# Issuing four small loads ahead of the entry barrier, beside the first two long ones

## The chip, the cores and the metric

The kernel runs on one core of a Trainium2 chip. The metric is the device time of one execution in microseconds. The kernel before takes 381.84 us (median of three runs, 381.80 to 381.89).

## The reference, cut to what matters

One decode step: attention of 32 query heads over a cache of 65,536 keys and values in 4 groups, and a gated mixer, both fed by the same row `x` of 1024 elements, and blended by a gate.

```python
g = _sigmoid((x * gate_w).sum(-1, keepdims=True))        # x and gate_w: 1024 elements each
a = _A_ref(x, A_k_cache, A_v_cache, A_wq, A_wo)          # x @ wq, scores, softmax, p @ v, @ wo
b = _B_ref(x, B_w_in, B_w_sp, B_b_sp, B_w_out)           # gelu, layernorm, * w_sp + b_sp, @ w_out
return g * a + (1 - g) * b
# ... the functions are left out; the sequence length is 1, so w_sp and b_sp are one number each
```

The weights and caches are 162 MB, all of which must be read once. `x`, `gate_w`, `w_sp` and `b_sp` together are about 4 KB.

## The kernel before

A recorder notes every operation with what it reads and writes, works out the waits, and emits each engine's instructions in program order. The long loads are issued by SP; those two that need no free slot are moved ahead of the entry barrier, the point near the start at which all engines wait for one another (`R.ahead = 2`). What one engine issues stands in one row of packets, which 16 transfer engines carry. A load is known to have landed by its semaphore: after its data, each transfer engine that took part sends a packet of 4 bytes, which the trace records like the others.

```python
        run("SP", nc.sync)
        # ...
        made = list(body.instructions)
        moved = made[first:first + self.ahead]
        body.instructions = made[:gate] + moved + made[gate:first] + made[first + self.ahead:]
        run("POOL", nc.gpsimd)
        run("PE", nc.tensor)
        run("ACT", nc.scalar)
        run("DVE", nc.vector)
```

The four small loads are ACT's first instructions, behind the barrier:

```python
    def small(dst, src, key):
        # ...
        P("ACT", f, w=[key], dma="l" + key)
    # ...
    small(xrow[0:8, 0:128], A_x[0, 0].rearrange("(i n) -> i n", i=8), KX)        # x: 8 rows of 256 bytes
    small(grow[0:8, 0:128], gate_w.rearrange("(i n) -> i n", i=8), KG)           # gate: the same
    small(wb[0:1, 0:1], B_w_sp, "wsp")                                           # 2 bytes
    small(wb[0:1, 1:2], B_b_sp.rearrange("(a n) -> a n", a=1), "bsp")            # 2 bytes
```

The long loads, in their order (8 MB, 8 MB, 7 MB and so on). A load is issued when the ring slots under it have been used up; `w_in` takes the slots of `wq`:

```python
    load([("wq", 0)], rows(A_wq, 0, 8), VB)
    load_k2(0, 0)
    load([("win", 0)], rows(B_w_in, 0, 8), VB)
    load_k(2, 2)
    # ... 25 more
```

PE's program in the first stage, in order: `x` turned into columns, the matmul that spreads `w_sp` and `b_sp`, the gate's matmul, then 64 matmuls on `wq`, after which the slots are free.

```python
    P("PE", f, r=["xm", "oneb"], w=[KTB])                      # x into columns
    # ...
    P("PE", lambda e: e.matmul(mb[:, 0:2], oneb[0:1, :], wb[0:1, :], start=True, stop=True),
      r=["oneb", "wsp", "bsp"], w=["mb"])
    # ... DVE: product of x and gate, its sum
    P("PE", lambda e: e.matmul(tb[:, 0:1], ones[0:8, :], col(C_GS)[0:8, :], start=True, stop=True),
      r=["ones", "gs"], w=[KTB])
    # ... the sigmoid
    wqs, keys = use(("wq", 0))
    # ...
    P("PE", f, r=["xT"] + keys, w=["ob"])                      # x @ wq
    done(("wq", 0))                                            # lets w_in be issued
```

## Time and profile before

| | before |
|---|---|
| time, us | 381.84 |
| span of the profile, us | 380.5 |
| share of the 16 transfer engines taken by the long loads | 98.8% |
| busiest compute engine | PE, 61% |
| last small load (`b_sp`) landed, us | 21.96 |
| first `wq` matmul, us | 23.51 |
| `w_in` issued, us | 29.46 |
| first keys transposed, us | 41.19 |

The third and fourth rows name the bound: bytes. The last four are the first stage, the one that the change touches. The lines of the page and of the timeline that show all this are in the prediction below. One view is not there: who waited for whom in the first 42 us of the kernel before (columns: total us, times, longest us).

```profile
PE mbt L430 <- DMA arena<-in_B_b_sp_dram: 10.5, 1, 10.5
...
DVE arena L495 <- DMA arena<-in_A_k_cache_dram: 9.0, 1, 9.0
...
DVE arena L420 <- DMA arena<-in_A_x_dram: 5.0, 1, 5.0
```

Three waits for transfers stand here. Two are for small loads, 10.5 and 5.0 us. The one in the middle, for the first keys, comes after both.

### The profile page before, as it was taken

How to read it: one execution, taken by the hardware profiler on the slowest of the kernel's cores; microseconds unless marked ns; L12 is line 12 of the kernel's file. 1: busy time of each engine (PE TensorE's matmuls, PEld its weight loads, DVE VectorE, ACT ScalarE, POOL GpSimd, SP SyncE). 2: the span in 40 equal slices, each digit the busy share in tenths (PEclk: the TensorE clock that was granted, in tenths of full speed). 3: DMA queues.
4: the chain of work that ended last, by engine and by line, in shares of the span. 5: the costliest groups of instructions: out<-in, count | busy, mean ns of one | idle time of the engine just before them, and what ended most of it. 6: DMA issues, size and time to landing. Idle time of an engine off the chain costs nothing.

```text
span 380.5 us, 2581 instructions
## 1 busy us (share of the span) xinstructions
PE 231.1 (61%) x1449; PEld 57.7 (15%) x836; DVE 204.1 (54%) x162; ACT 23.2 (6%) x24; POOL 8.4 (2%) x37
## 2 busy tenths in 40 slices
PE   0051488458548924894786128952895883738378
PEld 0010011011101200121111001220121110212015
DVE  3111596777389525955892249745875872322020
ACT  1000000010420000002100000022000000220010
POOL 5000000000000000000000000000000000000000
PEclk9998599696959985998799859995999897969789
DMA  9999999999999999999999999999999999999996
GB/s 441 434 406 400 469 388 437 441 483 417 415 406 434 441 436 427 441 420 424 474 434 441 441 441 406 408 434 441 434 417 432 441 441 434 436 410 431 417 424 252
DMA packets 4254, 162.17 MB, mean 426 GB/s; under 512 B 532, under 2 KB 532, under 8 KB 788
## 3 DMA queue, kind: packets, MB, share of 16 engines
q1 hardware_dynamic: 4208, 162.01, 98.8%
q8 instruction: 9, 0.15, 0.2%
q10 hardware_dynamic: 36, 0.00, 0.0%
q14 instruction: 1, 0.01, 0.0%
HBM read 162.01 MB, written 0.00 MB: 426 GB/s over the span
## 4 chain that ended last, share of the span: by engine, by line
DMA 57%; PE 21%; DVE 19%; ACT 1%; issue 1%; ACTq 0%; SPq 0%; DVEq 0%
DMA arena<-in_A_k_cache_dram 34%; DVE arena L495 17%; DMA arena<-in_A_wo_dram 10%; DMA arena<-in_A_v_cache_dram 8%; PE scp L253 5%; DMA arena<-in_B_b_sp_dram 5%; PE scp L255 5%; PE obt L253 4%; PE obt L255 4%; DVE arena L532 1%; PE fbt L705 1%; PE fbt L653 1%; ACT arena L527 1%; ACTq L281 0%; SPq L382 0%
## 5 line engine op out<-in xcount | busy, mean ns | idle before, releaser
L495 DVE STREAM_TRANSPOSE arena<-arena 128x2048 f32<-128x2048 f32 x64 | 142.6, 2281 | 45.4 <-DMA arena<-in_A_k_cache_dram 32.0
L253 PE MATMUL scp<-arena 128*128 128x512 bf16 (+1 forms) x275 | 110.7, 419 | 87.3 <-DVE arena L495 86.2
L255 PE MATMUL scp<-arena 128*128 128x512 bf16 (+1 forms) x279 | 110.5, 415 | 0.0
L253 PE MATMUL obt<-arena 128*64 128x512 bf16 (+2 forms) x334 | 62.3, 416 | 21.7 <-DMA arena<-in_A_v_cache_dram 20.3
L255 PE MATMUL obt<-arena 128*64 128x512 bf16 (+2 forms) x334 | 61.6, 411 | 0.0
L253 PEld LDWEIGHTS scp<-arena 128*128 128x128 bf16 (+1 forms) x275 | 27.3, 103 | 196.5 <-issue 96.9
L532 DVE STREAM_TRANSPOSE arena<-arena 128x2048 bf16<-128x2048 bf16 x7 | 16.2, 2311 | 30.1 <-PE obt L255 27.9
L253 PEld LDWEIGHTS obt<-arena 128*64 128x64 bf16 (+1 forms) x334 | 18.1, 112 | 74.3 <-issue 54.9
L527 ACT ACTIVATE arena<-arena 128x2048 bf16<-128x2048 f32 x8 | 16.0, 2002 | 218.7 <-DVE arena L524 195.8
L512 DVE TENSOR_SCALAR_CACHE_REDUCE arena<-scp 128x2048 f32<-128x2048 f32 x8 | 18.3, 2292 | 16.0 <-PE scp L255 16.0
L573 PE MATMUL mbt<-arena 128*128 128x128 bf16 x16 | 1.8, 243 | 12.6 <-DVE arena L568 12.6
L561 DVE RECIPROCAL arena<-mbt 128x1 f32<-128x1 f32 x4 | 0.6, 139 | 15.8 <-PE mbt L556 15.8
L524 DVE TENSOR_REDUCE arena<-mbt 128x1 f32<-128x32 f32 x4 | 0.8, 192 | 15.3 <-PE mbt L521 15.3
L483 POOL COPY arena<-arena 32x32 bf16<-32x32 bf16 x16 | 3.2, 203 | 235.5 <-PE scp L255 209.4
L535 DVE STREAM_TRANSPOSE arena<-arena 128x1024 bf16<-128x1024 bf16 x2 | 2.5, 1245 | 11.0 <-PE obt L255 11.0
L425 PE MATMUL scp<-arena 8*128 8x1 bf16 x8 | 0.7, 199 | 10.9 <-DVE arena L420 10.9
L430 PE MATMUL mbt<-arena 1*128 1x2 bf16 x1 | 0.2, 158 | 10.5 <-DMA arena<-in_B_b_sp_dram 10.5
L768 DVE CAST arena<-fbt 36x128 bf16<-36x128 f32 x1 | 0.3, 282 | 10.8 <-PE fbt L705 10.8
L432 DVE COPY arena<-mbt 128x2 f32<-128x2 f32 x1 | 0.2, 159 | 10.5 <-PE mbt L430 10.5
L705 PE MATMUL fbt<-arena 128*32 128x128 bf16 x128 | 4.1, 220 | 0.1
L420 DVE TENSOR_TENSOR arena<-arena 8x1024 bf16<-8x1024 bf16 x1 | 1.2, 1214 | 5.0 <-DMA arena<-in_A_x_dram 5.0
L460 DVE CAST arena<-obt 97x1024 bf16<-97x1024 f32 x1 | 1.2, 1225 | 5.0 <-PE obt L255 5.0
(91 smaller groups left out, 57.3 us busy)
## 6 DMA issues: line engine op xcount, KB each, us to landing
arena<-in_A_k_cache_dram SPq DMA_DIRECT2D x6, 4096.0 KB, 33.5
arena<-in_A_v_cache_dram SPq DMA_DIRECT2D x2, 4096.0 KB, 25.8
arena<-in_B_w_in_dram SPq DMA_DIRECT2D x1, 7168.0 KB, 29.9
arena<-in_A_wo_dram SPq DMA_DIRECT2D x3, 2048.0 KB, 33.2
arena<-in_B_w_out_dram SPq DMA_DIRECT2D x1, 3584.0 KB, 21.3
arena<-in_A_wo_dram SPq DMA_DIRECT2D x1, 1280.0 KB, 31.7
arena<-in_A_wo_dram SPq DMA_DIRECT2D x1, 512.0 KB, 32.5
arena<-in_A_wo_dram SPq DMA_DIRECT2D x1, 256.0 KB, 32.2
```

What stands on the lines that cost most here:

```text
L253: return e.matmul(*a, **kw)
L255: one = e.matmul(*a, **kw).ins
L420: P("DVE", lambda e: e.tensor_tensor(vw(xm, 0, [[128, 8], [1, 128]], 0, 8), vw(xrow, 0, [[0, 8], [1, 128]], 0, 8), vw(idb, 0, [[1, 8], [0, ...
L483: P("POOL", lambda e, pb=pb: e.tensor_copy(vw(qpad, 24 + 32 * pb, [[QP, 4], [1, 8]], 32 * pb, 32), vw(qall, 8 * g, [[32, 4], [1, 8]], 32 * ...
L495: P("DVE", lambda e: e.transpose(ktb(i).bitcast(F32), sl[:, 4096 * p:4096 * (p + 1)].bitcast(F32)), r=keys[4 * p:4 * p + 4], w=[("kt", i % ...
L512: P("DVE", lambda e: e.tensor_scalar(scs(j), scp[:, :], 0.0, None, op0=ALU.add, op1=ALU.max, accum_out=maxc[:, j:j + 1]), w=[("sc", j % 2) ...
L527: P("ACT", lambda e: e.activation(psb2, scs(j), ACTF.Exp, bias=gcol(j // 2, K_NB), scale=SCALE, accum_out=lp[:, j:j + 1]), r=[("sc", j % 2 ...
L532: P("DVE", lambda e: e.transpose(ptsb2, psb2), r=["psb"], w=[("ptsb", 0), ("ptsb", 1)])
L535: P("DVE", lambda e: e.transpose(ptsb(n), ab("PSB", 1024, 1024 * (n % 2))), r=["psb"], w=[("ptsb", n % 2)])
L573: ins = e.matmul(mb[:, 0:128], sel[:, 128 * c:128 * (c + 1)], osc[:, 128 * c:128 * (c + 1)], start=(c == 0), stop=(c == 3))
L653: ins = e.matmul(fb[32 * b:32 * (b + 1), 0:QW], e4z[0:97, 31 - j:63 - j], part[0:97, QW * s:QW * (s + 1)], start=(first and s % (NW // 2) ...
L705: ins = e.matmul(fb[32 * b:32 * (b + 1), 0:QW], ovz[:, z:z + 32], sl[:, o:o + QW], start=False, stop=(i == 3 and c == 7), tile_position=(0 ...
```

## The change

The intent: the small loads are issued beside the first two long loads rather than after the barrier, so that they land sooner and PE need not wait for `b_sp` when `wq` is already there. This is the whole diff.

```diff
--- before.py
+++ after.py
@@ -26,6 +26,7 @@
         self.readers = {}
         self.dma_count = {}
         self.ahead = 0
+        self.early = 0
 
     def op(self, eng, fn, r=(), w=(), dma=None):
         o = Op()
@@ -125,7 +126,13 @@
         body.instructions = made[:gate] + moved + made[gate:first] + made[first + self.ahead:]
         run("POOL", nc.gpsimd)
         run("PE", nc.tensor)
+        first = len(body.instructions)
         run("ACT", nc.scalar)
+        made = list(body.instructions)
+        gate = next(i for i, x in enumerate(made) if isinstance(x, mybir.InstDrain) and x.engine == mybir.EngineType.Activation)
+        moved = made[first:first + self.early]
+        assert all(isinstance(x, mybir.InstDMACopy) for x in moved)
+        body.instructions = made[:gate] + moved + made[gate:first] + made[first + self.early:]
         run("DVE", nc.vector)
 
 
@@ -769,6 +776,7 @@
     store()
 
     R.ahead = 2
+    R.early = 4
     R.emit(nc)
```

Nothing else moves. Lines of the changed kernel have numbers 7 higher in what follows (L430 becomes L437, L253 L260, L382 L389, L495 L502).

## The prediction

> **What bounds the kernel now.** I read the profile page first, then the chain of waits, the start and the end of the timeline, and the windows. The page's slices:
>
> ```profile
> PE 231.1 (61%) x1449; PEld 57.7 (15%) x836; DVE 204.1 (54%) x162; ACT 23.2 (6%) x24; POOL 8.4 (2%) x37
> ...
> DMA  9999999999999999999999999999999999999996
> ...
> q1 hardware_dynamic: 4208, 162.01, 98.8%
> q10 hardware_dynamic: 36, 0.00, 0.0%
> ```
>
> The reader is to see that no compute engine is busy for more than 61%, that the transfer engines are busy in every slice but the last, and that one queue (q1, the long loads) takes 98.8% of all they have. The small loads are q10: 36 packets, no measurable share. The transfer records of the trace, packet by packet, say the same more sharply: q1's first packet starts at 1.0 us, and from about 2 us to about 376 us all 16 engines have a packet in hand. 162.01 MB in 373 us is 434 GB/s. So the time is a sum of three terms: 1.0 us until the first byte, about 377 us of an unbroken stream, and 2.6 us of tail after the last slice of wo has landed (378.43 us last matmuls, 378.94 us the copy, 379.25 us the store). The 381.84 us of the clock is 1.3 us above the span of 380.5 us; I keep that difference.
>
> The start, from the timeline:
>
> ```profile
> 0.00 0.37 SPq L382 DMA_DIRECT2D arena<-in_A_wq_dram  x1
> ...
> 0.43 0.42 SPq L382 DMA_DIRECT2D arena<-in_A_k_cache_dram  x1
> 1.25 0.58 ACTq L281 DMA_DIRECT2D arena<-in_A_x_dram  x1
> ...
> 1.86 0.28 ACTq L281 DMA_DIRECT2D arena<-in_gate_w_dram  x1
> ...
> 9.63 1.21 DVE L420 TENSOR_TENSOR arena<-arena 8x1024 bf16<-8x1024 bf16 x1 [5.00 <-DMA arena<-in_A_x_dram]
> ...
> 22.09 0.16 PE L430 MATMUL mbt<-arena 1*128 1x2 bf16 x1 [10.54 <-DMA arena<-in_B_b_sp_dram]
> ...
> 23.51 0.60 PE L253 MATMUL obt<-arena 128*1 128x512 bf16 x4
> ...
> 29.46 0.33 SPq L382 DMA_DIRECT2D arena<-in_B_w_in_dram  x1
> ```
>
> The two long loads leave ahead of the barrier, at 0.00 and 0.43 us; the four small ones leave after it, from 1.25 us, and the last (b_sp, two bytes) lands at 2.47 + 19.49 = 21.96 us, its wait taken from the chain. PE runs in order: its tiny matmul of b_sp (L430) stands before the 64 matmuls on wq, with the gate's matmul (L437) between. wq landed at 21.8 us (page, issue to landing). So PE could begin on wq at about 21.9 us, and begins at 23.51 us. That 1.6 us is what the change is after.
>
> What stands behind it:
>
> ```profile
> 41.19 4.50 DVE L495 STREAM_TRANSPOSE arena<-arena 128x2048 f32<-128x2048 f32 x2 [8.96 <-DMA arena<-in_A_k_cache_dram]
> ```
>
> When q is ready (32 to 33 us), the kernel waits 8.96 us more for the first keys, which land at about 41 us whatever the compute did.
>
> **What the Trainium skill says.** All of it on the page "DMA: Bandwidth & Descriptors".
> 1. Section "Queues, rings and completion order": SP and ACT each own one row of rings on the same 16 engines, and an engine goes round-robin between rows, a whole packet at a time. The trace agrees: q1's packets are 65,536 bytes and take 2.42 us each; x's data packets start at 6.50 us, its semaphore packets at 8.93, gate's data at 11.35 and its semaphores at 13.78, w_sp's at 16.52 and 18.93, b_sp's at 21.36 us. Every small load pays two long packets, 4.84 us: one before its data, one before its semaphore. That is why two bytes need 19.5 us.
> 2. Section "Why a DMA increments its semaphore by 16 and not by 1": a transfer is split over the engines by its outer dimension, from the lowest engine up. The trace agrees: x and gate have 8 data packets each, w_sp and b_sp one each, so the four lie one behind the other on one engine's ring.
> 3. Section "Issuing engines are not separate DMA queues": issuing from several engines saves only the sequencer's issue time. No run here shows yet whether two sequencers that issue at once hinder each other; that is my main risk.
> 4. Section "Where 436 GB/s comes from": the ports carry 435.2 GB/s. The 434 GB/s above is there already, so the stream itself has nothing left to give.
>
> **The change part by part.**
> - Nothing is added or removed; the order of every engine's instructions but ACT's is the same, and on ACT four issues move across the barrier.
> - ACT's issues: 0.58 + 0.28 + 0.27 + 0.27 = 1.40 us. The raw trace shows the other engines reaching the barrier's drains from 0.12 to 0.31 us, and SP, the last, at 0.90 us, after its own two issues. If ACT begins at about 0.1 us, it gets to its drain at about 1.5 to 1.6 us and becomes the last. So the barrier opens about 0.65 us later, 1.9 us instead of 1.25 us. That delays the first memsets of POOL and DVE. DVE's preparation ends at 4.63 us now and at about 5.3 us then; it had 5.00 us of idle time before L420, so this costs nothing unless x lands before 5.3 us.
> - x is issued some 1.1 us earlier. Its packets now fall in behind two long packets (1.0 to 4.1 and 4.1 to 6.5 us). I expect them one long packet earlier, at about 4.1 us, perhaps two. The later ones follow at 4.84 us each, so b_sp lands at about 21.96 - 2.42 = 19.5 us (17.1 us if two). That is before wq's 21.8 us in either case.
> - So L430 and the gate's chain finish before 21.8 us, and PE's matmuls on wq start at about 21.9 instead of 23.51 us: 1.6 us earlier. Their own time, 23.51 to 29.46, stays near 5.9 us, and SP issues w_in at about 27.8 instead of 29.46 us.
> - What that is worth: at 29.46 us q1 still holds the rest of the first 8 MB of keys, landing at about 41 us, so w_in's issue has 11 us to spare and starts to move bytes at the same instant. On the compute side the 8.96 us wait grows to about 10.6 us. Later issues have slack as well: the fastest 8 MB load from issue to landing is 28.05 us (issued at 117.60 us), and 8.39 MB at 434 GB/s take 19.3 us, so about 8.7 us of work lay ahead of it in the queue. Gain at the end: 0.
> - The sum: 1.6 us gained in the first stage, 1.6 us given back in the wait for the first keys, 0 on the stream. Predicted 381.8 us.
>
> **The rivals.**
> *The 1.6 us reaches the end*, 380.2 us. For it: the chain of waits does lead through b_sp (5.1% of the span) and on into w_in's issue. Against it: the chain names what released each step last, not whether the queue was empty; all 16 engines had a packet in hand throughout, so issuing earlier only lengthens the queue. I give this 3% or so.
>
> *The small issues hinder the first long load.* Now SP has the first microsecond to itself: wq's packets start at 1.0 us on the first engine and 1.9 us on the last. If descriptors of both sequencers are made one at a time, ACT's four issues could push wq's packets back by up to their own 1.40 us, and since the stream never pauses, each bit of that goes to the end: at most 383.2 us. Against it: each is small (8 rows or one) and only those issued before about 0.4 us can precede wq. An estimate of 0 to 0.3 us, which I centre as 0.1 us and round away.
>
> *The small loads stay hidden or late*: if x still falls behind two long packets, b_sp lands where it did and even the first stage does not move. The time is again 381.8 us.
>
> *The later barrier becomes a bound*: 0.65 us of delay for POOL and DVE. It could only matter if x came first, and even then the work up to the gate has until 21.8 us. Nothing at the end.
>
> **Range and chances.** All likely ways end within 0.5 us of 381.8 us. The times of the kernel before lie within 0.09 us of each other, but another occasion or chip may differ by some tenths of a per cent, and the hindrance at the start is only upward. So the range is 381.2 to 382.5 us. A change of 2% would be 7.6 us, and nothing here is that large: faster 0.01, same 0.98, slower 0.01.
>
> **What would show it.** In the changed kernel's timeline: ACT's four issues within the first 1.7 us; POOL's first memset of the kernel (1.25 us before) at about 1.9 us; L420 starting at about 7.2 us (4.8 us at the least); L430 well before 21 us and waiting for b_sp no later than 19.5 us; the first wq matmul at about 21.9 us with wq as its releaser; w_in issued at about 27.8 us; the first key transpose still at 41.2 us, with its idle time near 10.6 us; and the tail unmoved, final store at 379.3 us. The prediction is wrong if q1's first packets start later than 1.0 to 1.9 us (then the end moves by the same amount), or if the first key transpose and the final store move up together, which would mean that the stream had a gap that I did not see.

## The result

| | before | after |
|---|---|---|
| time, us, median (range), 6 runs each | 381.82 (381.70 to 382.01) | 381.78 (381.65 to 381.91) |
| ratio after to before, 95% interval | | 0.9999 (0.9986 to 1.0012) |

A ratio is the mean time of one kernel's fast runs over that of the other's of the same rounds, so it is not quite the ratio of the medians.

The page of the changed kernel has the same two lines on the transfers; the long loads' share is 98.9% instead of 98.8%.

```profile
DMA  9999999999999999999999999999999999999996
...
q1 hardware_dynamic: 4208, 162.01, 98.9%
```

The timeline of its start (start us, duration us, engine, line, operation, and in brackets the idle time before it and what ended it):

```profile
0.00 0.37 SPq L389 DMA_DIRECT2D arena<-in_A_wq_dram  x1
0.12 0.56 ACTq L288 DMA_DIRECT2D arena<-in_A_x_dram  x1
...
1.34 0.27 ACTq L288 DMA_DIRECT2D arena<-in_B_b_sp_dram  x1
...
2.12 0.20 POOL L270 MEMSET arena<- 128x128 f32 x1 [1.71 <-POOLq L794]
...
7.42 1.22 DVE L427 TENSOR_TENSOR arena<-arena 8x1024 bf16<-8x1024 bf16 x1 [1.92 <-DMA arena<-in_A_x_dram]
...
21.67 0.16 PE L437 MATMUL mbt<-arena 1*128 1x2 bf16 x1 [12.32 <-DMA arena<-in_B_b_sp_dram]
...
28.93 0.33 SPq L389 DMA_DIRECT2D arena<-in_B_w_in_dram  x1
...
41.32 4.50 DVE L502 STREAM_TRANSPOSE arena<-arena 128x2048 f32<-128x2048 f32 x2 [9.63 <-DMA arena<-in_A_k_cache_dram]
```

The reader is to see four things. The small loads are issued from 0.12 us, and the barrier opens later (POOL's first memset of the kernel at 2.12 us instead of 1.25). `x` is used 2.21 us earlier (7.42 instead of 9.63). Yet `b_sp` is used only 0.42 us earlier (21.67 instead of 22.09): PE's idle time before it even grew, from 10.54 to 12.32 us. And the 0.53 us by which `w_in` is issued sooner (28.93 instead of 29.46) are gone at the next wait: the first keys are transposed at 41.32 us, with 9.63 us of idle time in place of 8.96.

The end moves by no more than the runs scatter. The last two steps of the changed kernel:

```profile
378.79 0.28 DVE L775 CAST arena<-fbt 36x128 bf16<-36x128 f32 x1 [11.04 <-PE fbt L712]
379.10 0.31 SPq L366 DMA_DIRECT2D out_dram<-arena  x1
```

They stand at 378.94 and 379.25 us in the kernel before: 0.15 us of difference, where the six runs of the changed kernel alone differ by 0.26 us.

**Why b_sp hardly moved.** The trace's transfer records, packet by packet, on the one engine that carries all four small loads (the records carry no engine number, so this engine was picked out by packets that start where another ends):

```
before                                         after
18.94 - 21.36  wq, 65,536 bytes (last one)     16.27 - 18.69  wq, 65,536 bytes
21.36          b_sp, 2 bytes                   18.69          b_sp, 2 bytes
21.36          wq's semaphore, 4 bytes         18.69 - 21.11  wq, 65,536 bytes (last one)
21.37          b_sp's semaphore, 4 bytes       21.11          b_sp's semaphore, 4 bytes
```

In the kernel before, `b_sp`'s two bytes came up right behind the last long packet of `wq`. The long row's next packet was then `wq`'s own semaphore of 4 bytes, so `b_sp`'s semaphore waited about 0.01 us for its turn. In the changed kernel the two bytes come up one long packet sooner, and the semaphore then has to let that last long packet pass: 2.42 us. The one was gained at the data and lost at the semaphore. What is left, 0.26 us at the semaphore, is mostly the difference in where this engine's first long packet ended in the two executions (4.40 and 4.16 us). Another 0.17 us of the 0.43 us between the two landings (21.96 and 21.53 us) lies behind the semaphore's packet; no run explains it.

A data packet waits for its turn as a semaphore does: in the changed kernel gate's data, issued at 0.72 us, start on this engine at 9.00 us, one long packet after x's semaphore at 6.58 us. And other executions show how little the 0.43 us means: with the small loads after the barrier `b_sp` landed at 21.96 us and, in gate_after_wq below, at 21.68 us; with x or all four ahead of it, in the same order, at 21.51 to 21.72 us in six executions. That the change made `b_sp` land sooner at all is not clear of this scatter.

### The profile page after: what moved, and what is told of

It is laid out like the page before. It is cut to its first block, busy times and chain, and to the rows that moved or that the text cites. A ratio compares the mean times of both kernels' runs of the same rounds, so it can differ in the third digit from the quotient of the medians.

```text
span 380.3 us, 2581 instructions
## 1 busy us (share of the span) xinstructions
PE 235.1 (62%) x1449; PEld 58.1 (15%) x836; DVE 204.6 (54%) x162; ACT 23.3 (6%) x24; POOL 8.4 (2%) x37
## 3 DMA queue, kind: packets, MB, share of 16 engines
q1 hardware_dynamic: 4208, 162.01, 98.9%
## 4 chain that ended last, share of the span: by engine, by line
DMA 56%; PE 23%; DVE 18%; ACT 1%; issue 1%; SPq 0%; ACTq 0%; DVEq 0%
DMA arena<-in_A_k_cache_dram 34%; DVE arena L502 15%; DMA arena<-in_A_wo_dram 10%; DMA arena<-in_A_v_cache_dram 8%; PE scp L260 7%; PE scp L262 6%; DMA arena<-in_B_b_sp_dram 5%; PE obt L260 4%; PE obt L262 4%; DVE arena L539 1%; PE fbt L712 1%; PE fbt L660 1%; ACT arena L534 1%; SPq L389 0%; ACTq L288 0%
## 5 line engine op out<-in xcount | busy, mean ns | idle before, releaser
L502 DVE STREAM_TRANSPOSE arena<-arena 128x2048 f32<-128x2048 f32 x64 | 143.0, 2284 | 48.2 <-DMA arena<-in_A_k_cache_dram 32.7
L260 PE MATMUL scp<-arena 128*128 128x512 bf16 (+1 forms) x275 | 112.8, 429 | 87.7 <-DVE arena L502 86.3
L262 PE MATMUL scp<-arena 128*128 128x512 bf16 (+1 forms) x279 | 113.1, 427 | 0.0
L260 PE MATMUL obt<-arena 128*64 128x512 bf16 (+2 forms) x334 | 62.9, 419 | 17.5 <-DMA arena<-in_A_v_cache_dram 17.5
L260 PEld LDWEIGHTS scp<-arena 128*128 128x128 bf16 (+1 forms) x275 | 27.7, 104 | 200.1 <-issue 101.3
L260 PEld LDWEIGHTS obt<-arena 128*64 128x64 bf16 (+1 forms) x334 | 18.3, 113 | 70.7 <-issue 56.1
L437 PE MATMUL mbt<-arena 1*128 1x2 bf16 x1 | 0.2, 158 | 12.3 <-DMA arena<-in_B_b_sp_dram 12.3
L712 PEld LDWEIGHTS fbt<-arena 128*32 128x32 bf16 x128 | 3.6, 97 | 1.6 <-DMA arena<-in_A_wo_dram 0.8
```

Source lines behind the costliest of these rows:

```text
L260: return e.matmul(*a, **kw)
L262: one = e.matmul(*a, **kw).ins
L502: P("DVE", lambda e: e.transpose(ktb(i).bitcast(F32), sl[:, 4096 * p:4096 * (p + 1)].bitcast(F32)), r=keys[4 * p:4 * p + 4], w=[("kt", i % ...
L712: ins = e.matmul(fb[32 * b:32 * (b + 1), 0:QW], ovz[:, z:z + 32], sl[:, o:o + QW], start=False, stop=(i == 3 and c == 7), tile_position=(0 ...
```

## The experiments

Two questions: does a gain in the first stage reach the end at all, and is the turn-taking of packets what sets the landing of the small loads? The theory said no and yes. The rival: the change gave nothing only because `b_sp` was still late, and the 1.6 us would show in the time if the first stage really won them.

### x_only: only x ahead of the barrier

```diff
-    R.early = 4
+    R.early = 1
```

> Only x is issued ahead of the barrier; gate, w_sp and b_sp after it. Theory (each small load waits one long packet for its data and one for its semaphore, so only the head of the row matters): the later three still reach the rings before their turn, so x's data start at 4.1 us, gate's at 9.0, w_sp's at 13.9, b_sp's at 18.7 us as in the changed kernel, and the first wq matmul at 23.1 us. Rival (each load's own issue time matters): gate, w_sp and b_sp come as late as in the kernel before, b_sp's data at 21.4 us. Both: time 381.8 us.

Measured: 381.81 us (one run), kernel before 381.89 us. ACT issued x at 0.12 us and gate at 1.25 us, `w_sp` at 1.56, `b_sp` at 1.86. On the engine in question x's data started at 4.34 us, gate's at 9.19, `w_sp`'s at 14.04, `b_sp`'s at 18.88, and its semaphore at 21.30; the first `wq` matmul at 23.27 us. So the theory holds: moving one load does nearly what moving four does, because the others stand in the row behind x anyway. The first `wq` matmul comes 0.19 us later than in the changed kernel, as this engine's first long packet ended 0.18 us later (4.34 and 4.16 us).

### scalars_first: another order of the four

```diff
+    small(wb[0:1, 0:1], B_w_sp, "wsp")
+    small(wb[0:1, 1:2], B_b_sp.rearrange("(a n) -> a n", a=1), "bsp")
     small(xrow[0:8, 0:128], A_x[0, 0].rearrange("(i n) -> i n", i=8), KX)
     small(grow[0:8, 0:128], gate_w.rearrange("(i n) -> i n", i=8), KG)
-    small(wb[0:1, 0:1], B_w_sp, "wsp")
-    small(wb[0:1, 1:2], B_b_sp.rearrange("(a n) -> a n", a=1), "bsp")
```

> The changed kernel with the order of the four small loads changed: w_sp, b_sp, x, gate. Theory (four loads one behind the other on one engine, two long packets each): w_sp's data at 4.1 us, b_sp's at 9.0, x's on that engine at 13.9 and its semaphore at 16.3, gate's at 18.7 and 21.1; so the x product starts at about 16.7 us instead of 7.4 us, gate lands last at 21.5 us, and the first wq matmul stays near 23 us. Rival (small loads overtake one another by size or engine): x lands at 7 us as before. Time 381.8 us either way.

Measured: 381.67 us (one run). The row kept its order, but in this execution one thing was not as expected: `w_sp`'s data and semaphore both passed at 1.00 us, ahead of the first long packet. So it cost no long packet, and `b_sp`, issued at 0.67 us, started at 6.51 us, behind two of them. x landed at 14.19 us, gate at 19.05, each one long packet before my numbers. With that, everything small was there before `wq`:

```profile
19.07 0.28 DVE L440 TENSOR_TENSOR arena<-arena 8x128 f32<-8x128 bf16 x1 [2.66 <-DMA arena<-in_gate_w_dram]
...
21.97 0.60 PE L260 MATMUL obt<-arena 128*1 128x512 bf16 x4 [1.68 <-DMA arena<-in_A_wq_dram]
...
41.30 4.50 DVE L500 STREAM_TRANSPOSE arena<-arena 128x2048 f32<-128x2048 f32 x2 [10.21 <-DMA arena<-in_A_k_cache_dram]
```

The first `wq` matmul starts at 21.97 us, released by `wq`: the whole 1.54 us that the change was after, against the 23.51 us before. And the first keys are transposed when they always were. This start is not fixed: the same kernel, profiled again in scalars_first_timed below, did as expected.

### wq_halves: shorter packets beside the small loads

The changed kernel, with the load of `wq` cut into two of 4 MB each.

```diff
-    load([("wq", 0)], rows(A_wq, 0, 8), VB)
+    for hw in range(2):
+        load([("wq", hw)], rows(A_wq, 0, 8)[:, SUB * hw:SUB * (hw + 1)], VB + SUB * hw)
     ... (the matmuls take each half from its own load)
-    R.ahead = 2
+    R.ahead = 3
```

> The changed kernel with the wq load cut in two, so that its packets are 32 KB and take 1.21 us. Theory: each small load then waits about 2.4 us in place of 4.84, b_sp lands at 10 to 13 us, wq's landing (21.9 us) releases PE, the first wq matmul starts at about 22.0 us and w_in is issued at about 27.8 us, over 1 us earlier than in the changed kernel; the first key transpose stays at 41.2 us and the time at 381.8 us plus or minus 0.4. Rival (the change moved nothing only because b_sp was still late): the time falls by 1 to 1.6 us, to about 380.4 us.

Measured: 381.81 us (4 runs), kernel before 381.89; ratio 0.9999 (0.9984 to 1.0013). The packets of `wq` were 32,768 bytes and took 1.21 us. The last four small packets, data and semaphore of `w_sp` and `b_sp`, started at 7.77, 8.99, 10.20 and 11.42 us, one such packet apart, where the changed kernel has 13.85, 16.27, 18.69 and 21.11 us. `b_sp` landed at 11.82 us instead of 21.53, and PE waited for `wq` alone:

```profile
11.96 0.16 PE L438 MATMUL mbt<-arena 1*128 1x2 bf16 x1 [4.55 <-DMA arena<-in_B_b_sp_dram]
...
21.86 0.60 PE L260 MATMUL obt<-arena 128*1 128x512 bf16 x4 [8.41 <-DMA arena<-in_A_wq_dram]
...
28.12 0.33 SPq L390 DMA_DIRECT2D arena<-in_B_w_in_dram  x1
...
41.10 4.50 DVE L506 STREAM_TRANSPOSE arena<-arena 128x2048 f32<-128x2048 f32 x2 [10.21 <-DMA arena<-in_A_k_cache_dram]
```

Halving the packets halved the small loads' waits: the turn-taking is what sets their landing. And the first stage's gain, now 1.34 us at `w_in`'s issue (28.12 against 29.46), is worth nothing at the end. The rival's 380.4 us falls.

### gate_after_wq: the order of PE instead of the order of the loads

The kernel before, with the matmul of `w_sp` and `b_sp` and the gate's chain moved behind q in program order.

```diff
-    P("PE", lambda e: e.matmul(mb[:, 0:2], oneb[0:1, :], wb[0:1, :], start=True, stop=True),
-      r=["oneb", "wsp", "bsp"], w=["mb"])
-    ... (the gate's chain, 14 lines)
     wqs, keys = use(("wq", 0))
     ...
     P("DVE", lambda e: e.tensor_copy(qall, tb[:, 0:128]), w=["qall", KTB])
+    (the same lines)
```

> The kernel before (small loads after the barrier) with the matmul of b_sp and the gate's chain moved behind q in program order, so PE does not wait for b_sp ahead of wq. Theory: first wq matmul at about 21.9 us instead of 23.5 us, w_in issued at about 27.9 us, first key transpose still at 41.2 us, time 381.8 us plus or minus 0.4. Rival: the 1.6 us reaches the end, 380.2 us.

Measured: 381.94 us (4 runs), kernel before 381.89; ratio 1.0003 (0.9986 to 1.0019). The first `wq` matmul was released by `wq`, and the first keys did not move:

```profile
22.12 0.60 PE L253 MATMUL obt<-arena 128*1 128x512 bf16 x4 [10.63 <-DMA arena<-in_A_wq_dram]
...
28.22 0.33 SPq L382 DMA_DIRECT2D arena<-in_B_w_in_dram  x1
...
41.36 4.51 DVE L496 STREAM_TRANSPOSE arena<-arena 128x2048 f32<-128x2048 f32 x2 [8.24 <-DMA arena<-in_A_k_cache_dram]
```

Same finding by another road: the first stage won 1.4 us, the time nothing.

### small_on_sp_first: the small loads in front of everything

```diff
-        P("ACT", f, w=[key], dma="l" + key)
+        P("SP", f, w=[key], dma="l" + key)
-    R.ahead = 2
-    R.early = 4
+    R.ahead = 6
+    R.early = 0
```

> The four small loads go on the SP queue ahead of wq and the keys, all before the barrier. Theory (the stream never pauses, so its start is what counts): the first wq packet starts 1.2 to 1.5 us later, x lands at about 2 us and b_sp at about 3.5 us, the first wq matmul follows wq's landing at 23.1 to 23.4 us, and the time grows by about what the first packet lost, to 382.9 to 383.3 us. Rival (the start of the stream is hidden, the chain of waits counts): small loads out of the way, time 380.2 to 381.8 us.

Measured: 383.07 us (4 runs), kernel before 381.89; ratio 1.0032 (1.0017 to 1.0047), so 1.2 us slower; the interval leaves 1 out. x landed at 1.62 us and `b_sp` at 2.21 us, so no small load is waited for any more, and this is the only variant with the same bytes and work that is measurably slower:

```profile
1.33 0.36 SPq L389 DMA_DIRECT2D arena<-in_A_wq_dram  x1
...
7.63 0.16 PE L437 MATMUL mbt<-arena 1*128 1x2 bf16 x1
...
23.23 0.60 PE L260 MATMUL obt<-arena 128*1 128x512 bf16 x4 [14.03 <-DMA arena<-in_A_wq_dram]
...
42.53 4.51 DVE L502 STREAM_TRANSPOSE arena<-arena 128x2048 f32<-128x2048 f32 x2 [10.14 <-DMA arena<-in_A_k_cache_dram]
...
380.45 0.31 SPq L366 DMA_DIRECT2D out_dram<-arena  x1
```

`wq` is issued 1.33 us later, its first packet starts at 2.32 us instead of 1.00, the keys are there 1.3 us later, and the final store comes 1.2 us later than in the kernel before (379.25). What the head of the stream lost, 1.3 us, goes to the end almost whole, 1.2 us.

### delay_short and delay_long: idle matmuls ahead of wq

The changed kernel with 24, then 90, matmuls of no use on PE just ahead of the `wq` matmuls.

```diff
+    def f(e):
+        for k in range(24):          # delay_long: range(90)
+            ins = mm(e, k > 0, scp[:, 1024:1536], idb, ab("OVZ", 512), start=True, stop=True)
+        return ins
+    P("PE", f, r=["idb", ("ovec", 0)], w=[KTB])
     wqs, keys = use(("wq", 0))
```

> The changed kernel with 24 idle matmuls on PE just ahead of the wq matmuls, some 5 to 7 us of them. Theory (11 us of keys are still queued when w_in is issued): w_in's issue moves from 28.9 to about 34 us, the queue does not run dry, time within 0.4 us of 381.8. Rival (the chain from b_sp through wq to w_in's issue sets the end): time up by 5 us or more.

> The same with 90 idle matmuls, some 20 us. Theory: w_in is issued at about 48 us, the second load (keys) has ended at 41 us, so the queue is dry for about 7 to 8 us and the time grows by that, to 388 to 391 us, not by the full 19 us. Rival: the full delay, 400 us; or none at all if the queue has more slack than I read.

Measured, delay_short: 381.72 us (4 runs), kernel before 381.78; ratio 0.9997 (0.9980 to 1.0014). `w_in` was issued 5.8 us later than in the changed kernel, and nothing came of it:

```profile
34.75 0.33 SPq L389 DMA_DIRECT2D arena<-in_B_w_in_dram  x1
...
41.33 4.50 DVE L508 STREAM_TRANSPOSE arena<-arena 128x2048 f32<-128x2048 f32 x2 [3.82 <-DMA arena<-in_A_k_cache_dram]
```

Measured, delay_long: 391.89 us (4 runs, 391.10 to 392.35); ratio 1.0262 (1.0246 to 1.0277), 10.1 us slower. `w_in` was issued at 49.10 us, 20.2 us later than in the changed kernel, so half of the delay was hidden and half showed. The windows from 40 to 52 us, of the changed kernel and then of delay_long (busy time of each engine, its instructions, the granted clock, the transfer engines' busy share and GB/s), show where:

```profile
40.00:52.00 12.00, 7.64 (x25) 1.46 (x13) 9.12 (x5) 0.00 (x0) 0.00 (x0) 0.67 1.06 459
```

```profile
40.00:52.00 12.00, 9.82 (x102) 1.34 (x44) 1.84 (x4) 0.00 (x0) 0.07 (x1) 1.00 0.24 78
```

The share in these 12 us fell from 1.06 to 0.24 (a packet counts where it starts, hence the 1.06), which is 0.82 x 12 = 9.8 us of transfer lost. In the packet records no packet of a load was under way from 41.20 to 50.06 us (one packet of instructions was). That is the gap that the changed kernel never has: from 2 to 375 us the time in which transfer engines had no packet of a load adds up to 0.5 us of all 16, in delay_long (to 385 us) to 10.1 us. My expectation of 388 to 391 us was a little low: the queue was dry for about 9 us rather than 7 to 8, since `w_in`'s own first packets start another microsecond after its issue.

### extra_2mb: one more load

The changed kernel with 2 MiB more to read, into a slot that is free at the time and never looked at.

```diff
     load_k2(0, 0)
+    load([("extra", 0)], rows(A_wo, 0, 8), 2 * SUB)
+    used.add(("extra", 0))
     load([("win", 0)], rows(B_w_in, 0, 8), VB)
```

> The changed kernel with one more load of 2 MiB (a part of wo, never used) into a ring slot that is free, between the first keys and w_in. Theory (the bytes are the bound): 2.10 MB at 434 GB/s are 4.83 us, time 386.5 us plus or minus 0.5. Rival (compute chain is the bound): time within 1 us of 381.8.

Measured: 386.61 us (4 runs), kernel before 381.78, so 4.83 us more by the medians; ratio 1.0126 (1.0111 to 1.0141). To agree with the expected 4.83 us to the hundredth is luck, since the interval is 4.2 to 5.4 us; but the rival, at most 1 us, is out. The bytes are the bound.

### after_again and scalars_first_timed: five rounds each

> The changed kernel once more, timed in five rounds, to see a difference of a tenth of a per cent if there is one. Theory (stream of bytes is the bound, the head of it untouched): same as the kernel before to within 0.2 us. Rival: the 0.4 us that the first stage gained shows, 381.4 us.

> The order w_sp, b_sp, x, gate, timed in five rounds. In its first look the wq matmuls started at 21.97 us, released by wq itself, so the whole 1.5 us of the first stage is won. Theory: same as the kernel before to within 0.2 us. Rival: 1.1 to 1.5 us faster, 380.4 us.

Measured in the same rounds: kernel before 381.84 us (9 runs); changed kernel 381.86 us (5 runs), ratio 0.9999 (0.9985 to 1.0012); scalars_first 381.93 us (5 runs), ratio 1.0002 (0.9989 to 1.0014). Nothing of the first stage shows. How much that was varies, though. In the profiled execution of after_again the first `wq` matmul started at 23.26 us, 0.25 us before the 23.51 us. In that of scalars_first_timed it started at 22.73 us, a gain of 0.78 us in place of 1.54: here `w_sp`'s data passed at 4.21 us, behind the first long packet, not at 1.00 us, and all else stood where the expectation of scalars_first had it (`b_sp`'s data at 9.05 us, gate's semaphore at 21.17 us). So which packet passes first at the start differs between executions of one kernel, and these five rounds don't test a gain of 1.5 us; wq_halves and gate_after_wq do. No variant was measurably faster than the kernel before.

## Why the prediction was right, and where one step failed

- **The bound.** Right. extra_2mb cost what its bytes take, small_on_sp_first cost nearly what it delayed the first packet, delay_long cost about what the queue was dry, and the rest cost nothing. One figure is off: the prediction divides by 373 us to get 434 GB/s, but the loads' packets run from 1.00 to 377.97 us, which gives 430 GB/s; 16 packets of 65,536 bytes in 2.42 us are 433 GB/s. Nothing rests on the difference.
- **The issues and the barrier.** Right in kind: ACT began at 0.12 us, as read from the drains. The barrier opened 0.87 us later instead of the 0.65 us named. DVE's last preparation then ended at 5.50 us, before x at 7.4 us, and so it cost nothing.
- **x one long packet earlier.** Right: its data started at 4.11 us on the first engine, and the product at 7.42 us (7.2 named). Why it is one and not two stays open: x, issued at 0.12 us, came behind one long packet, while `b_sp` in scalars_first, issued at 0.67 us, came behind two.
- **"So b_sp lands at about 21.96 - 2.42 = 19.5 us".** This is the step that failed: it landed at 21.53 us. The sum took 4.84 us for each small load throughout, one long packet before the data and one before the semaphore. But in the kernel before, `b_sp` had not paid the second, because its data came up just as `wq` ended; the numbers quoted in the prediction already say so, since data at 21.36 us and a landing at 21.96 us leave no room for another 2.42 us between them. The changed kernel paid it. (The prediction's list of starts also mixes engines: x's and gate's are those of the first of eight, and on the engine of `w_sp` and `b_sp` they are 6.82, 9.25, 11.67 and 14.10 us. Its steps of 2.42 us are the same.)
- **The first wq matmul at 21.9 us, w_in at 27.8 us.** Wrong as a consequence: 23.08 and 28.93 us. wq_halves (21.86 and 28.12), scalars_first (21.97 and 28.33) and gate_after_wq (22.12 and 28.22) show that the reading of what `wq` itself allows was right.
- **The gain given back in the wait for the first keys.** Right, with a smaller gain: that wait grew to 9.63 us, not 10.6; in scalars_first and wq_halves it grew to 10.21. For this reason the time at the end could not tell the failed step from a correct one: a gain of 0.4 us or of 1.6 us is taken by the same wait.
- **11 us to spare at w_in's issue.** Right: 5.8 us of delay were free, and of 20.2 us about 10 were.
- **Two sequencers at once hinder each other.** Not seen: the first packets of the 16 engines started from 0.99 to 1.58 us in the changed kernel and from 1.00 to 1.91 us in the kernel before.

Why the time is the same is therefore shown, not only argued: with three different edits the first stage won 1.4 to 1.65 us at its first `wq` matmul in the profiled execution, and the time did not move; nor did it when `w_in` was issued 5.8 us later. What was only read from records of single executions is the order of packets on one engine; wq_halves supports it by its size.

## What to carry to other kernels

In this kernel the transfer queue never runs dry, and what changed the time was when its first byte started (small_on_sp_first), how many bytes it carried (extra_2mb) and a gap in it (delay_long). What is left to do after the last byte should count too; no run changed it. A wait that a transfer ended was worth nothing here as long as the queue was not empty. So before moving a small load, count how many long packets it must let pass on its engine, its semaphore included, and see whether the next wait would take the gain anyway. Putting small loads in front of the stream to save a wait behind it cost 1.2 us here.

## What the Trainium skill lacked or had wrong

- Page "DMA: Bandwidth & Descriptors", section "Queues, rings and completion order": it says that an engine switches rows at packet boundaries, and counts a packet in descriptors, but not how long a packet can take. Here a packet of the long row was the contiguous piece of one partition: 65,536 bytes and 2.42 us, or 32,768 bytes and 1.21 us where the load was cut in two. A small load's data and its semaphore each waited for one or two of these, in a few cases for none.
- Same page, section "Why a DMA increments its semaphore by 16 and not by 1": it has the semaphore's increment as each engine's last descriptor, landing after that engine's data, but not that a small load's semaphore takes its own turn behind a long packet of another row. In the changed kernel this made 2.42 us for `b_sp`, and in the kernel before 0.01 us, where the other row's next packet was itself a semaphore.
- Same page, no section: that the order at the start, when two engines issue at once, can differ between executions of one kernel. In scalars_first `w_sp`'s data passed at 1.00 us, in scalars_first_timed, the same kernel, at 4.21 us.
- Same page, section "Latency and other measured facts": it has about 0.6 us to the first byte without saying from when. Here the first packet started 1.00 us after the start of the issue of `wq`, which took 0.37 us, so 0.63 us after its end.
